# Reordering the steps of a fused attention and expert kernel before its expert work begins

## The chip, the cores and the metric

The kernel runs on one core of a Trainium2 chip. TensorE multiplies matrices into PSUM, VectorE and ScalarE work elementwise and reduce, GpSimd (POOL) does small vector work and issues some DMAs, SyncE (SP) issues the others. Each engine works through its own instructions in the order in which the program gives them, and engines wait for each other by semaphores. The metric is device time in microseconds; lower is better.

## The reference

```python
scores = scale * np.matmul(q, k.transpose(0, 1, 3, 2))
thresh = np.max(scores, axis=-1, keepdims=True) - tau
scores = np.where(scores >= thresh, scores, -1000000000.0)
scores = scores - np.max(scores, axis=-1, keepdims=True)
attn = np.exp(scores)
attn = attn / (np.sum(attn, axis=-1, keepdims=True) + 1e-09)
attn_out = np.matmul(attn, v)
x = attn_out.transpose(0, 2, 1, 3).reshape(B * S, H * D)
h = x @ w_in
out = np.maximum(0.01 * h, h) @ w_out
```

q, k and v have 8 batches, 8 heads, 576 rows and 64 columns; tau is 0.02. An attention in which only scores within tau of their row's maximum count is followed by two products (512 by 2048, 2048 by 512) with a leaky ReLU between them, the "expert" part.

## The kernel before, in words

Two heads make a pair, and two pairs a couple; there are 16 couples (c0 to c15), two to a batch. A couple is worked in 9 steps (t0 to t8) of 128 query rows for two heads. I write c1 t3 for step 3 of couple 1. One more round of 9 steps, with no attention of its own, ends the program.

What a step issues, by function:

- `s_mm(c, t)` (L158): TensorE's scores for both heads, each as three float16 products (high by high, low by high, high by low), into two tiles of two PSUM banks. There are only two such tiles, so the scores of the next step wait until this step's have been read.
- `s_max(c, t, h, direct)`: VectorE copies the negated scores of head h to SBUF and takes the row maximum (L181); POOL adds tau (L186). Then either ScalarE takes the exponential `e` (L191), and the threshold is applied later by VectorE, or, where `direct` is set, ScalarE makes the masked weights itself, in two instructions: `far` (L197), which drives values beyond the threshold far down, and an exponential into `W` with the row sum (L201).
- `s_mask(c, t)`: VectorE multiplies `e` by the threshold test (L214) for each head that was not direct, with the row sum; SP then issues the DMA that transposes `W` into `wT` (L220). It is called one step after its `s_max`. There are six `W` buffers.
- `prep(p, i)`: TensorE transposes q or k of a coming pair (L129) into the pair of banks with the tag "A", of which there is one; ScalarE makes the high half (`hi`, L138), VectorE the rest (`lo`, L139). The latter is put in a list, `soon`, and issued at the end of the step.
- `sums_0` to `sums_4`: the inverse row sums of a finished couple. POOL adds 1e-9 (L228), VectorE takes the reciprocal (L234), POOL and VectorE split it into two float16 parts (L235, L240), TensorE turns it (`sums_3`, L246) and spreads it over rows (`sums_4`, L263), each into the banks "A"; ScalarE copies the results to SBUF (`row`, L249; `rc`, L268).
- `values(c, e)`: 20 products of the transposed weights and v into the banks "A" (L279); at the end of the step VectorE multiplies by the inverse sums (L289) and POOL copies a strip (L293).

Expert work comes in units: `h_unit` (four 512-column products, L301, and the leaky ReLU on ScalarE, L305) and `out_mm` (four products with `w_out`, L316; every fourth ends a sum that ScalarE copies out). `push_main(b)` puts the 32 units of a batch in a list, 16 of the first kind and then 16 of the second. That happens at t6 of every even couple from c2 on, when the batch's second couple has been multiplied with v. `work(n)` issues the next n units. How many a step gets is computed from a table of shares and from the units and steps that remain, with a carried credit. Steps before c2 t6 have none.

POOL also issues the DMAs that load v (`load_v`) and, one per step from step 1 to 32, the slices of `w_in` and then `w_out` (`load_w`, L105 and L109); a step's number is 9c + t. SP issues the loads of q and k (L81, L86).

The order of the calls in a step, before: `s_mm`; `values` of the previous couple in t3 and t5; `s_max` of head 0, never direct; half the units; `prep`; `sums_4` in t2 and t4; `s_max` of head 1, which in couples 0 to 2 is direct except in t3 and t7; the other half of the units (in t1 `sums_1` to `sums_3` lie among these); `s_mask` of the previous step; `soon`; `sums_0` in t0; the DMAs.

Of the kernel before, what the change touches and what calls it, by code (L numbers as in the profile page):

```python
# [16 lines left out]
def kernel(  # L17
# [10 lines left out]
    nc = tc.nc  # L28
    B, H, S, D = q.shape
    tau_f = float(tau)  # L30
# [4 lines left out]
    NT = 9  # L35
# [10 lines left out]
    I16 = sb.tile([128, 128], FP16, name="I16")  # L46
# [3 lines left out]
    sel = sb.tile([128, 18, 64], FP16, name="sel")  # L50
# [19 lines left out]
    def bank():  # L70
        return ps.tile([128, 512], FP32, tag="u", bufs=2, name="u")
# [39 lines left out]
    soon = []  # L111

    def take(fs):
        r = list(fs)
        fs.clear()
        return r

    def run(fs):
        for f in fs:
            f()  # L120

    def prep(p, i, tag="A", bufs=1):
# [12 lines left out]
        N = 512 + 128 * i  # L135
        hi = sb.tile([128, N], FP16, tag=f"hi{i}", bufs=3, name=f"hi{i}")
        lo = sb.tile([128, N], FP16, tag=f"lo{i}", bufs=3, name=f"lo{i}")
        nc.scalar.activation(out=hi[:, :], in_=pt[:, 0:N], func=AF.Copy, bias=0.0, scale=QS)  # L138
        soon.append(lambda: nc.vector.scalar_tensor_tensor(  # L139
            out=lo[:, :], in0=pt[:, 0:N], scalar=QS, in1=hi[:, :],  # L140
            op0=OP.mult, op1=OP.subtract,
        ))
        qk.setdefault(p, {})[i] = (hi, lo)
# [88 lines left out]
    def sums_1(c):  # L232
        d1, rr = inv[c]
        nc.vector.reciprocal(out=rr[:, :], in_=d1[:, :])  # L234
        nc.gpsimd.tensor_scalar(out=r2[:, 0, 0:18], in0=rr[:, :], scalar1=1.0 / RS, scalar2=0.0,  # L235
                                op0=OP.mult, op1=OP.add)

    def sums_2(c):
        d1, rr = inv[c]
        nc.vector.scalar_tensor_tensor(out=r2[:, 1, 0:18], in0=rr[:, :], scalar=1.0 / RS, in1=r2[:, 0, 0:18],  # L240
                                       op0=OP.mult, op1=OP.subtract)
# [29 lines left out]
    def values(c, e):  # L271

        b, g = divmod(2 * c + e, NG)
        wT, vb = wTs[c], Vs[b % 2]
        t = pair_of_banks()
        for half in range(2):
            for kb in range(5):
                for h in range(2):
                    nc.tensor.matmul(  # L279
                        out=t[ds(h * 64, 64), half, 0:288], lhsT=vb[:, g, h, kb, :],  # L280
                        rhs=wT[:, 4 * h + kb, ds(e * 576 + half * 288, 288)],
                        start=(kb == 0), stop=(kb == 4), skip_group_check=True,
                    )
        rc = rcs.pop(e)
        x = sb.tile([128, 576], FP16, tag=f"xT{g}", bufs=2, name=f"xT{g}")
        xTs[(b, g)] = x

        def mul():
            nc.vector.tensor_tensor(  # L289
                out=x.rearrange("p (a b) -> p a b", a=2), in0=t[:, :, 0:288],  # L290
                in1=rc.rearrange("p (a b) -> p a b", a=2), op=OP.mult,
            )
            nc.gpsimd.tensor_copy(out=xE[g][:, b, :], in_=x[:, 0:64] if e else x[:, 512:576])  # L293
        soon.append(mul)
# [15 lines left out]
    def out_mm(key, g_in, part, osb, half, store):  # L310
# [9 lines left out]
        if part == 3:  # L320
# [6 lines left out]
                nc.scalar.activation(out=o[:, half, :], in_=t[:, :], func=AF.Copy, bias=0.0, scale=1.0)  # L327
            store(o)

    units = []  # L330

    def new_osb():
# [42 lines left out]
    def work(n):  # L375
        for _ in range(min(n, len(units))):
            units.pop(0)[1]()

    with tc.manual_schedule():
        nc.scalar.preload_act_table_set("natural_log_exp_and_others")  # L380
        for i, tail in ((0, 0), (1, 0), (0, 1), (1, 1)):
            load_qk(0, i, tail)
        make_identity(nc, I32)
        nc.vector.tensor_copy(out=I16[:, :], in_=I32[:, :])
        nc.vector.memset(ntau[:, :], -tau_f)
        nc.vector.memset(r2[:, :, :], 0.0)
        nc.vector.tensor_tensor(
            out=sel[:, :, :], in0=I32[:, 0:18].unsqueeze(2).to_broadcast([128, 18, 64]),
            in1=I32[:, 64:82].unsqueeze(2).to_broadcast([128, 18, 64]), op=OP.add,
        )  # L390
        nc.vector.tensor_scalar(out=sel[:, :, :], in0=sel[:, :, :], scalar1=RS, scalar2=None, op0=OP.mult)
        for t in Vs:
            nc.vector.memset(t[64:128, :, 0, 4, :], 0.0)
            nc.vector.memset(t[0:64, :, 1, 0, :], 0.0)
        for p in range(1, 3):
            for i in range(2):
                for tail in range(2):
                    load_qk(p, i, tail)
        prep(0, 0)
        prep(0, 1, "s", 2)  # L400
        run(take(soon))
        share = (23, 27, 23, 13, 23, 13, 23, 23, 23)
        credit = 0.0
        w_at = [1 + i for i in range(32)]
        prev = None
        for c in range(NC + 1):
            last = c == NC
            for t in range(NT):
                step = c * NT + t
                if c > 1 and c % 2 == 0 and t == 6:  # L410

                    if c % 4 == 2 and c > 2:
                        push_tail(c // 2 - 3, 1)
                    push_main(c // 2 - 1)
                    if c % 4 == 0:
                        push_tail(c // 2 - 2, 0)
                    if last:
                        push_tail(c // 2 - 2, 1)
                if not last:
                    s_mm(c, t)  # L420


                nxt = {6: (2 * c + 2, 0), 7: (2 * c + 2, 1), 8: (2 * c + 3, 0), 0: (2 * c + 1, 1)}
                if c == 0:
                    nxt[0], nxt[1] = (1, 0), (1, 1)
                pi = nxt.get(t)
                if pi is not None and pi[0] >= NP:
                    pi = None
                if c == 0 and t < 2:
                    prep(*pi)  # L430
                    pi = None

                if c > 0 and t in (3, 5):
                    values(c - 1, t // 2 - 1)

                ahead = [share[i % NT] for i in range(step, (c // 2 * 2 + (0 if c % 2 == 0 and t < 6 else 2)) * NT + 6)]
                credit = min(credit, 1.0) + (len(units) - credit) * share[t] / sum(ahead)
                n = min(int(credit + 0.01), len(units))
                credit -= n
                if not last:  # L440


                    direct = tau_f <= 16.0 and (
                        t not in (3, 7) if c < 3 else t in (3, 5) or not any(u[0] for u in units[:n]))
                    s_max(c, t, 0, False)
                if c > 0 and t == 1:
                    sums_1(c - 1)
                work(n - n // 2)
                if pi is not None:
                    prep(*pi)  # L450
                if c > 0 and t in (2, 4):
                    sums_4(c - 1, t // 2 - 1)
                if not last:
                    s_max(c, t, 1, direct)
                if c > 0 and t == 1:
                    sums_2(c - 1)
                    work(n // 2 - 1)
                    sums_3(c - 1)
                    work(1 if n > 1 else 0)
                else:  # L460
                    work(n // 2)
                if prev is not None:
                    s_mask(*prev)
                    prev = None
                if not last:
                    prev = (c, t)
                run(take(soon))
                if c > 0 and t == 0:
                    sums_0(c - 1)
                if c == 0 and 0 < t < 6:  # L470
                    load_v(0, t - 1)
                if c % 2 == 0 and c > 0 and t >= 4 and c // 2 < B:
                    load_v(c // 2, t - 4)
                for i in range(32):
                    if w_at[i] == step:
                        load_w(i)
                if t < 4 and 2 * c + 3 < NP:
                    load_qk(2 * c + 3, t // 2, t % 2)
                elif 4 <= t < 8 and 2 * c + 4 < NP:
                    load_qk(2 * c + 4, t // 2 - 2, t % 2)  # L480
        work(len(units))
# [35 lines left out]
```

## Time and profile before

| what | value |
|---|---|
| median of 3 runs | 539.75 us (538.6 to 540.45) |
| the profiled execution | 540.02 us, span 538.3 us |
| mean granted TensorE clock | 0.967 |
| busy: PE, DVE, ACT, POOL | 497.8, 421.7, 433.8, 188.1 us |
| start of the first maximum: c0 t0, c1 t0, c2 t0, c2 t6 | 10.13, 36.49, 64.60, 82.99 us |

The profile lists one execution. PE is TensorE's matmuls, PEld its weight loads, DVE VectorE, ACT ScalarE, SPq and POOLq the queues of SyncE and GpSimd; L181 is line 181 of the kernel, and `sn<-s` means that tile `sn` is written from tile `s`. A mark like `[0.74 <-PE s L158]` behind an instruction says that its engine sat idle for 0.74 us before it, and what ended that. A couple takes 26.36 and 28.11 us (c0, c1), then 28.68 (c2), and from c3 on 29.7 to 30.8 us.

Starts of the steps before the first expert unit, as lengths from one first maximum to the next:

| | t0 | t1 | t2 | t3 | t4 | t5 | t6 | t7 | t8 |
|---|---|---|---|---|---|---|---|---|---|
| c0 | 2.92 | 2.94 | 2.35 | 2.92 | 2.92 | 2.91 | 2.92 | 3.05 | 3.43 |
| c1 | 2.93 | 3.58 | 2.98 | 3.64 | 2.84 | 2.77 | 2.94 | 3.00 | 3.43 |
| c2 | 2.93 | 3.58 | 2.99 | 3.28 | 2.84 | 2.77 | | | |

### The profile page before, as it was taken

To read this page: it belongs to the slowest core of one execution; us is meant where nothing else is said; L and a number is where in the kernel's file an instruction comes from. 1 tells how busy PE (TensorE), PEld (TensorE's weight loads), DVE (VectorE), ACT (ScalarE), POOL (GpSimd) and SP (SyncE) were. 2 spreads that over 40 slices of the span, in tenths; PEclk is the share of its full clock that TensorE was granted. 3 is DMA by queue.
4 is the path that set the end of the run, shared out by engine and by line. 5 is a ranking of instruction groups with operands and counts; after the bars stand their busy time and mean duration, and the time that the engine had idled before them with its cause. 6 is when DMAs were issued, how large, how long until landed. Compare 5 with 4: busy or idle time off the path is not lost.

```text
span 538.3 us, 12333 instructions
## 1 busy us (share of the span) xinstructions
PE 497.8 (92%) x4384; PEld 272.8 (51%) x4384; DVE 421.7 (78%) x1106; ACT 433.8 (81%) x765; POOL 188.1 (35%) x430
## 2 busy tenths in 40 slices
PE   5678679899999999999999999999999999999996
PEld 3345454454545565454545566455545566445444
DVE  4897989988899878987899878987899878982000
ACT  3887879899878989889888989889888989884622
POOL 0754556443433334222432234323432234331000
PEclk9676969999999999999999999999999999999999
DMA  6999999998998699778999799777998699654001
GB/s 151 150 202 161 175 182 214 200 180 173 172 165 136 139 169 196 140 137 153 183 155 143 132 182 185 142 135 159 183 155 136 132 187 135 111 89 106 39 40 58
DMA packets 266814, 80.50 MB, mean 150 GB/s; under 512 B 251905, under 2 KB 264193, under 8 KB 266753
## 3 DMA queue, kind: packets, MB, share of 16 engines
q1 hardware_dynamic: 249136, 70.68, 72.3%
q0 software_dynamic: 17536, 8.92, 14.2%
q8 instruction: 34, 0.56, 0.4%
q14 instruction: 28, 0.22, 0.1%
q10 hardware_dynamic: 80, 0.13, 0.1%
HBM read 36.70 MB, written 9.44 MB: 86 GB/s over the span
## 4 chain that ended last, share of the span: by engine, by line
PE 43%; ACT 25%; DVE 16%; issue 8%; DMA 4%; POOL 3%; SPq 0%; DVEq 0%; ACTq 0%; POOLq 0%
PE u L316 13%; DVE sn L181 11%; PE u L301 10%; PE s L158 10%; PE A L279 8%; ACT e L191 7%; ACT far L197 5%; ACT W L201 5%; DVE W L214 3%; ACT gM L305 3%; ACT hi L138 3%; POOL nth L186 3%; DMA nat<-in_q_dram 2%; DVE lo L139 1%; ACT rc L268 1%
## 5 line engine op out<-in xcount | busy, mean ns | idle before, releaser
L181 DVE TENSOR_SCALAR_CACHE_REDUCE sn<-s 128x576 f32<-128x576 f32 x288 | 206.5, 750 | 49.3 <-PE s L158 49.1
L186 POOL TENSOR_SCALAR nth<-nmx 128x1 f32<-128x1 f32 x288 | 127.4, 442 | 251.7 <-DVE sn L181 229.5
L191 ACT ACTIVATE e<-sn,nmx 128x576 f16<-128x576 f32 x196 | 150.5, 769 | 32.4 <-DVE sn L181 32.2
L214 DVE SCALAR_TENSOR_TENSOR W<-sn,nth,e 128x576 f16<-128x576 f32 x196 | 155.6, 814 | 0.0
L301 PE MATMUL u<-xT,win 128*128 128x512 f16 x512 | 128.9, 380 | 2.5 <-ACT gM L305 2.5
L316 PE MATMUL u<-wout,gM 128*128 128x512 f16 x512 | 126.2, 380 | 0.0
L158 PEld LDWEIGHTS <-hi 64*128 64x128 f16 (+1 forms) x1280 | 65.1, 99 | 70.2 <-issue 54.9
L158 PE MATMUL s<-hi,hi 64*128 64x288 f16 x512 | 86.2, 300 | 10.3 <-DVE sn L181 8.8
L158 PE MATMUL s<-lo,hi 64*128 64x288 f16 (+1 forms) x640 | 92.2, 294 | 0.0
L158 PE MATMUL s<-hi,lo 64*128 64x288 f16 (+1 forms) x640 | 92.1, 294 | 0.0
L301 PEld LDWEIGHTS <-win 128*128 128x128 f16 x768 | 58.7, 98 | 56.5 <-issue 20.1
L305 ACT ACTIVATE gM<-u 128x512 f16<-128x512 f32 x128 | 74.6, 588 | 11.7 <-PE u L301 11.7
L197 ACT ACTIVATE far<-sn,nth 128x576 f32<-128x576 f32 x92 | 71.0, 771 | 13.8 <-POOL nth L186 11.6
L201 ACT ACTIVATE W<-far,ntau 128x576 f16<-128x576 f32 x92 | 71.3, 775 | 3.0
L316 PEld LDWEIGHTS <-gM 128*128 128x128 f16 x512 | 44.7, 98 | 51.3 <-issue 12.3
L139 DVE SCALAR_TENSOR_TENSOR lo<-A,hi 128x512 f16<-128x512 f32 (+1 forms) x63 | 47.6, 756 | 14.2 <-ACT hi L138 13.7
L129 PE MATMUL A<-I,nat 128*128 128x128 f32 x283 | 44.6, 288 | 9.9 <-DVE lo L139 4.7
L279 PE MATMUL A<-wT,V 128*64 128x288 f16 x640 | 47.5, 297 | 1.5 <-ACT rc L268 1.1
L129 PEld LDWEIGHTS A<-I,nat 128*128 128x128 f32 x283 | 35.2, 147 | 25.2 <-DVE lo L139 10.0
L138 ACT ACTIVATE hi<-A 128x512 f16<-128x512 f32 (+1 forms) x63 | 40.0, 636 | 7.6 <-PE A L129 7.6
L279 PEld LDWEIGHTS <-V 128*64 128x64 f16 x640 | 36.6, 113 | 11.9 <-issue 8.4
L158 PEld LDWEIGHTS <-lo 64*128 64x128 f16 (+1 forms) x640 | 32.1, 99 | 12.6 <-issue 8.9
(44 smaller groups left out, 292.1 us busy)
## 6 DMA issues: line engine op xcount, KB each, us to landing
nat<-in_q_dram SPq DMA_DIRECT2D x32, 256.0 KB, 3.8
nat<-in_k_dram SPq DMA_DIRECT2D x32, 256.0 KB, 3.9
out_dram<-osb SPq DMA_DIRECT2D x16, 512.0 KB, 3.0
wT<-W SPq DMA_TRANSPOSE x144, 3.9
V<-in_v_dram POOLq DMA_DIRECT2D x8, 256.0 KB, 6.1
win<-in_moe_w_in_dram POOLq DMA_DIRECT2D x16, 128.0 KB, 5.2
V<-in_v_dram POOLq DMA_DIRECT2D x16, 128.0 KB, 4.7
wout<-in_moe_w_out_dram POOLq DMA_DIRECT2D x16, 128.0 KB, 4.3
```

What stands on the lines that cost most here:

```text
L129: nc.tensor.matmul(out=pt[0:128, ds(c * 128, 128)], lhsT=t[0:128, 4 * i + c, :, :].rearrange("p h d -> p (h d)"), rhs=I32[:, :], is_transp ...
L158: nc.tensor.matmul(out=out[h][po, half, 0:288], lhsT=qk[p][i][a][r, cols], rhs=qk[p][1][b][r, ds(half * 288, 288)], start=(ti == 0), stop= ...
L181: nc.vector.tensor_scalar(out=sn[:, h, :].rearrange("p (a b) -> p a b", a=2), in0=s_[:, :, 0:288], scalar1=-BS, scalar2=None, op0=OP.mult, ...
L186: nc.gpsimd.tensor_scalar(out=nth[:, h:h + 1], in0=nmx[:, h:h + 1], scalar1=1.0, scalar2=tau_f, op0=OP.mult, op1=OP.add,)
L191: nc.scalar.activation(out=e[:, h, :], in_=sn[:, h, :], func=AF.Exp, bias=nmx[:, h:h + 1], scale=-1.0,)
L197: nc.scalar.activation(out=far[:, :], in_=sn[:, h, :], func=AF.Prelu, bias=nth[:, h:h + 1], scale=-1.0, alpha=BIG,)
L201: nc.scalar.activation(out=w[:, ds(h * 576, 576)], in_=far[:, :], func=AF.Exp, bias=ntau[:, 0:1], scale=1.0, accum_out=dens[c][:, 2 * t + ...
L214: nc.vector.scalar_tensor_tensor(out=w[:, ds(h * 576, 576)], in0=sn[:, h, :], scalar=nth[:, h:h + 1], in1=e[:, h, :], op0=OP.is_le, op1=OP ...
L279: nc.tensor.matmul(out=t[ds(h * 64, 64), half, 0:288], lhsT=vb[:, g, h, kb, :], rhs=wT[:, 4 * h + kb, ds(e * 576 + half * 288, 288)], star ...
L301: nc.tensor.matmul(out=t[:, ts(j, N)], lhsT=w_in16[:, gi, ts(j0 + j, 128)], rhs=xs[gi], start=(gi == 0), stop=(gi == NG - 1), skip_group_c ...
L305: nc.scalar.activation(out=g_out, in_=t[:, 0:nj * N].rearrange("p (j n) -> p j n", j=nj), func=AF.Prelu, bias=0.0, scale=1.0, alpha=0.01)
L316: nc.tensor.matmul(out=t[:, :], lhsT=g_in(j), rhs=w_out16[:, j, :], start=(j == 0), stop=(j == NJ - 1), skip_group_check=True,)
```

## The change

Steps up to c2 t3 get an order of their own ("early"); all later steps keep the old one, without the parts that belonged to the earlier couples.

- `prep` is issued right behind `s_mm`, ahead of both maxima, so that ScalarE's `hi` stands ahead of the step's exponentials.
- Head 0 is direct in every early step, head 1 never. VectorE masks one head per step.
- The chain of sums and values of couple 0 takes t0 to t4 of couple 1, that of couple 1 takes t0 to t3 of couple 2: `sums_0`; then `sums_1` and `sums_2` one behind the other; a step later `sums_3` and `sums_4` of the first pair; then `values` of the first pair; then `sums_4` and `values` of the second. `sums_3` and the second `sums_4` stand ahead of the step's maxima, the first `sums_4` and both `values` behind the mask.
- In c1 t8 the mask of that step is issued in the step itself, behind that of the step before.
- A new function, `keep_busy`, issues 5 products of 512 columns (3 in steps with a `prep`) into a bank that nobody reads, at the end of each early step but the three that hold sums and values.
- The units of batch 0 are pushed at c2 t4 instead of t6, and the shares are spread over 20 steps instead of 18. In c2 t4 to t8 head 1 is direct in t5, and elsewhere only where the step has no `h_unit`.
- The weight slices are loaded in steps 4 to 33 (two of them in steps 4 and 19) instead of 1 to 32.

```diff
+    def keep_busy(n):
+        t = bank()
+        for _ in range(n):
+            nc.tensor.matmul(
+                out=t[:, :], lhsT=I16[:, :], rhs=sel[:, 0:8, :].rearrange("p a b -> p (a b)"),
+                start=True, stop=True, skip_group_check=True,
+            )
...
-        w_at = [1 + i for i in range(32)]
+        w_at = [4 + 94 * i // 100 for i in range(32)]
...
-                if c > 1 and c % 2 == 0 and t == 6:
+                if c > 1 and c % 2 == 0 and t == (4 if c == 2 else 6):
...
+                early = c < 2 or c == 2 and t < 4
+                if early:
+                    u = t - (0 if c == 2 else 1) if c > 0 else None
+                    if pi is not None:
+                        prep(*pi)
+                    if u == 1:
+                        sums_3(c - 1)
+                    if u == 3:
+                        sums_4(c - 1, 1)
+                    s_max(c, t, 0, tau_f <= 16.0)
+                    s_max(c, t, 1, False)
+                    if prev is not None:
+                        s_mask(*prev)
+                    prev = (c, t)
+                    if c == 1 and t == 8:
+                        s_mask(*prev)
+                        prev = None
+                    if c == 1 and t == 0 or c == 2 and t == 0:
+                        sums_0(c - 1)
+                    if u == 0:
+                        sums_1(c - 1)
+                        sums_2(c - 1)
+                    if u == 1:
+                        sums_4(c - 1, 0)
+                    if u in (2, 3):
+                        values(c - 1, u - 2)
+                    run(take(soon))
+                    if u not in (1, 2, 3):
+                        keep_busy(5 if pi is None else 3)
...
-                ahead = [share[i % NT] for i in range(step, (c // 2 * 2 + (0 if c % 2 == 0 and t < 6 else 2)) * NT + 6)]
+                    ahead = [share[i % NT] for i in range(
+                        step, (c // 2 * 2 + (0 if c % 2 == 0 and c > 2 and t < 6 else 2)) * NT + 6)]
...
-                    direct = tau_f <= 16.0 and (
-                        t not in (3, 7) if c < 3 else t in (3, 5) or not any(u[0] for u in units[:n]))
+                        direct = tau_f <= 16.0 and (t in (3, 5) or not any(u[0] for u in units[:n]))
```

More of the change, by code (lines that the diff above doesn't have):

```diff
@@ L428 @@
                     pi = None
[L429 to L434, printed above, removed]
-                ahead = [share[i % NT] for i in range(step, (c // 2 * 2 + (0 if c % 2 == 0 and t < 6 else 2)) * NT + 6)]
-                credit = min(credit, 1.0) + (len(units) - credit) * share[t] / sum(ahead)
-                n = min(int(credit + 0.01), len(units))
-                credit -= n
@@ L440 @@
-                if not last:
-                    direct = tau_f <= 16.0 and (
-                        t not in (3, 7) if c < 3 else t in (3, 5) or not any(u[0] for u in units[:n]))
[L445 to L459, printed above, removed]
-                else:
[L461 to L469, printed above, removed]
+                early = c < 2 or c == 2 and t < 4
@@ new lines @@
+                if early:
[26 more added lines that the diff above has]
+                        keep_busy(5 if pi is None else 3)
+                else:
+                    if c > 2 and t in (3, 5):
+                        values(c - 1, t // 2 - 1)
+                    ahead = [share[i % NT] for i in range(
+                        step, (c // 2 * 2 + (0 if c % 2 == 0 and c > 2 and t < 6 else 2)) * NT + 6)]
+                    credit = min(credit, 1.0) + (len(units) - credit) * share[t] / sum(ahead)
+                    n = min(int(credit + 0.01), len(units))
+                    credit -= n
+                    if not last:
+                        direct = tau_f <= 16.0 and (t in (3, 5) or not any(u[0] for u in units[:n]))
+                        s_max(c, t, 0, False)
+                    if c > 2 and t == 1:
+                        sums_1(c - 1)
+                    work(n - n // 2)
+                    if pi is not None:
+                        prep(*pi)
+                    if c > 2 and t in (2, 4):
+                        sums_4(c - 1, t // 2 - 1)
+                    if not last:
+                        s_max(c, t, 1, direct)
+                    if c > 2 and t == 1:
+                        sums_2(c - 1)
+                        work(n // 2 - 1)
+                        sums_3(c - 1)
+                        work(1 if n > 1 else 0)
+                    else:
+                        work(n // 2)
+                    if prev is not None:
+                        s_mask(*prev)
+                        prev = None
+                    if not last:
+                        prev = (c, t)
+                    run(take(soon))
+                    if c > 2 and t == 0:
+                        sums_0(c - 1)
```

## The prediction

> **What bounds the kernel now.** I read the slices first, then busy time by stage, then the engines' instructions in order of time inside the first stage. The page's slices, 13.5 us each, come first.
>
> ```profile
> PE   5678679899999999999999999999999999999996
> ...
> PEclk9676969999999999999999999999999999999999
> ```
>
> Nearly all of TensorE's idle time, and all of its reduced clock, lies in the first nine slices. The stretches are cut at the start of steps c0 t0, c1 t0, c2 t0 and c2 t6 (the first step with an expert unit); columns: length, then PE, PEld, DVE, ACT, POOL busy, clock, DMA share, GB/s.
>
> ```profile
> 10.13:36.49 26.36, 19.74 (x143) 11.29 (x142) 23.75 (x62) 21.16 (x36) 15.48 (x31) 0.74 1.13 166
> 36.49:64.60 28.11, 19.29 (x190) 12.10 (x190) 25.14 (x67) 22.56 (x40) 14.10 (x31) 0.82 1.18 177
> 64.60:82.99 18.39, 14.33 (x132) 9.10 (x133) 16.03 (x45) 14.40 (x26) 9.67 (x21) 0.72 1.07 187
> 82.99:142.67 59.68, 56.47 (x508) 29.78 (x507) 51.14 (x135) 53.99 (x99) 27.71 (x61) 1.00 1.11 183
> 142.67:484.00 341.33, 334.13 (x3083) 182.85 (x3083) 296.87 (x781) 297.98 (x528) 118.67 (x274) 1.00 0.88 152
> ```
>
> From 83 us TensorE is busy 95 to 98%: there the time is its work. Before that no engine is full; the limit is a loop, seen in two neighbouring steps of VectorE:
>
> ```profile
> 15.99 0.75 DVE L181 TENSOR_SCALAR_CACHE_REDUCE sn<-s 128x576 f32<-128x576 f32 x1
> ...
> 18.34 0.76 DVE L181 TENSOR_SCALAR_CACHE_REDUCE sn<-s 128x576 f32<-128x576 f32 x1 [0.17 <-PE s L158]
> 19.02 0.08 DVE L181 DVE_READ_ACCUMULATOR sn<-s 128x1 f32 x1
> 19.02 0.76 DVE L181 TENSOR_SCALAR_CACHE_REDUCE sn<-s 128x576 f32<-128x576 f32 x1
> ...
> 21.26 0.76 DVE L181 TENSOR_SCALAR_CACHE_REDUCE sn<-s 128x576 f32<-128x576 f32 x1 [0.74 <-PE s L158]
> ```
>
> Two maxima (0.68 us apart) free the score banks, then TensorE computes the next scores. With the clock up a step takes 2.35 us (15.99 to 18.34), with it halved 2.92 (18.34 to 21.26). ScalarE's row for the direct mask follows.
>
> ```profile
> 18.24 0.78 ACT L197 ACTIVATE far<-sn,nth 128x576 f32<-128x576 f32 x1
> 19.05 0.77 ACT L201 ACTIVATE W<-far,ntau 128x576 f16<-128x576 f32 x1
> 19.73 0.18 ACT L201 ACTIVATION_READ_ACCUMULATOR W<-far,ntau 128x1 f32 x1
> 19.82 1.42 ACT L191 ACTIVATE e<-sn,nmx 128x576 f16<-128x576 f32 x2
> ```
>
> Spacings: far 0.80, W 0.87 with its accumulator read, e 0.67: one direct and one indirect head cost 2.34 us of ScalarE per step, as much as the 2.35 us loop.
>
> **The change, part by part.** I write S for the start of a step's first maximum. Up to c2 t3 every step now has head 0 direct, head 1 by e and a mask. Head 0's maximum ends at S+0.76, the threshold takes 0.19 (POOL's row beside a maximum; 0.70 beside a mask), so far starts at S+1.1, W at 1.9, e at 2.77, ending at S+3.44. That is 1.1 us into the next step. ScalarE is thus always half a step behind VectorE, and it matters in three places below.
>
> *c0 t0 and t1.* Three fillers come after each prep. A 512-column product costs 0.215 us (four in 0.86). With the clock low I take 0.43, because the 288-column pairs go from 0.12 apart to 0.24. At t0 the clock is low until about 14.4: 3 x 0.43 = 1.3 us in front of the next scores, of which VectorE's own order hides 0.3. **+1.0.**
> *c0 t2 to t5.* Before 2.35 + 3 x 2.92 = 11.1. Five fillers (1.08) fit in the 1.42 us that TensorE waits for the two maxima and keep it 85% busy, so the clock stays. ScalarE and the loop both give 2.36; I take 2.38, 9.5 in all. **-1.6.** If the fillers failed to hold the clock, it would be 0.
> *c0 t6 to c1 t0, four preps.* Before 12.33. VectorE: 1.36 maxima + 0.74 mask + 0.61 or 0.74 lo; ScalarE: 2.34 + 0.5 to 0.6 hi: 2.75, 2.88, 2.75, 2.95 = 11.33 (t7's second mask is gone). **-1.0.**
> *c1 t1, t2.* Before 3.58 + 2.98. The reciprocal and its rounding are now back to back: VectorE waits for one POOL result (0.3) but TensorE's turn, a step later, no longer waits ahead of the scores. 2.97 + 2.40. **-1.2.**
> *c1 t3 to t5.* The row sums' copy to SBUF (rc, 0.63) is issued after e in t2, so on ScalarE it ends 1.7 us into t3. Values need the same pair of banks, so they start at S+1.76; behind them, in TensorE's order, wait the next scores and all of VectorE's next step. Clock up: 1.76 + 1.35 (20 products) + 0.9 scores = 4.0; t4 (sums 0.42, rc 0.63, values 1.35, scores 0.9) 3.4; t5 2.4. Sum 9.8. Clock halved: values 2.4, scores 1.5, five fillers 2.1: 12.9 if it lasts. Before: 9.25. There are no fillers here, and between the scores of t2 and the values TensorE has 1.6 us of work (0.27 + 0.42 + 0.9) in 4.8. The nearest row is c1 t1 of before, TensorE in order of time and then the stretches around it:
>
> ```profile
> 38.48 0.53 PE L158 MATMUL s<-lo,hi 64*128 64x288 f16 x2
> 41.12 0.29 PE L246 MATMUL A<-I,r 128*128 128x128 f16 x1 [2.11 <-DVE r L240]
> ```
>
> ```profile
> 31.30:41.10 9.80, 5.10 (x58) 3.11 (x57) 9.67 (x28) 8.22 (x14) 4.86 (x12) 0.85 1.25 240
> 41.10:48.50 7.40, 6.58 (x50) 4.17 (x50) 5.06 (x14) 6.09 (x11) 3.65 (x7) 0.50 1.16 171
> ```
>
> After an idle stretch of 2.11 us the clock was 0.50 for 7.4 us. So I take 11.9, nearer to the low clock. **+2.6** (0.5 to 3.7).
> *c1 t6, t7.* 5.94 to 5.63. **-0.3.**
> *c1 t8: couple 1's own last mask at once.* It waits for e of its own step: ScalarE hi, far, W, e end at S+4.2. The mask ends at 5.0, lo of the next prep behind it at 5.62, and only then the next maximum. Before 3.43. **+2.2.** TensorE meanwhile waits 3.2 us for lo to free the transposes' banks.
> *c2 t0.* No mask is left (-0.74), but the chain POOL, reciprocal, POOL, rounding stands on VectorE ahead of lo (3.5 in all), and with the clock low transposes 1.26 + fillers 1.29 + scores 1.5 give 4.05. Before 2.93. **+1.1** (0.6 to 1.1).
> *c2 t1 to t3.* As in couple 1: 2.4 + 4.0 + 3.4 = 9.8 at full clock, 12.3 at half; 11.0 taken, as TensorE comes in busy from t0. Before 9.85. **+1.1** (0 to 2.5).
> *c2 t4, t5, now with a unit each.* Masks on VectorE bind; 5.4 for 5.61. **-0.2.**
> Start of c2 t6: 1.0 - 1.6 - 1.0 - 1.2 + 2.6 - 0.3 + 2.2 + 1.1 + 1.1 - 0.2 = **+2.7**, between +0.5 and +5.
>
> *Two units done early.* The shares give one unit in t4, one in t5, and 30 instead of 32 up to c4 t5. 2 x 0.86 us of TensorE, of which the share that it is busy there (56.47 of 59.68) counts: **-1.6** (-1.0 to -1.7).
> *The weight loads.* SP's order keeps its DMAs; POOL's loads of weights now end in step 33 instead of 32, while the output unit that reads the last slices moves from step 35 to 34. Before, issue at 113.53 and use at 119.44 were 5.9 us apart; the time to landing of these loads (L109):
>
> ```profile
> DMA to landing us min/median/max: 3.2/4.3/6.8
> ```
>
> Now the issue is at S+2.2 of c3 t6, the use at S+4.1 (a step of 3.3, then three products). TensorE waits 1.3 to 4.9, by the median 2.4, in a stretch where it is the bound: **+2.4** (0 if landing is quicker than any row).
>
> Sum: 2.7 - 1.6 + 2.4 = +3.5. The profiled execution took 540.02 (span 538.3 and 1.7 around it), 0.27 above the median 539.75; 543.5 there is **543.2** as a median.
>
> **The rivals.**
> *The clock stays up in the chains* (fillers just before them, none within). c1 t3 to t5 then cost +0.5 and c2 t1 to t3 nothing: +0.5 - 1.6 + 2.4 = +1.3, **541.0**, no change. For it: 48.5 to 66 us had the clock at 0.99 with TensorE busy 67%. Against: the 2.11 us row. The Trainium skill, page TensorE: Matmul & The Clock Gate, section "Why this matters for your kernels", asks for no idle gap over about 3 us; by that rule the gaps of 1.8 us here would keep the clock, and this rival would hold. The trace disagrees: 2.11 us preceded 0.50.
> *Faster: ScalarE is not behind.* If e of head 1 ends by the second maximum (S+1.4), t8's mask waits for nothing (-2.9), values start 1.4 sooner twice, and c2 t0 loses its low clock (-0.55): 0.5 - 2.9 - 2.8 - 0.55 = -5.8, and -5.0 in all, **534.7**. It decides where ScalarE's step is under about 2.0 us. For it: ScalarE was busy only 80% in couple 0. Against: 0.80 + 0.87 + 0.67 leaves it no slack to catch up with.
> *Slower still: the turning DMAs of W are late.* SP issued almost without a pause from 19.6 to 77 us; couple 0's last transfer was issued at 39.91 and by the median of 5.0 landed at 44.9, where values could now start at 45.0. At the longest landing, 9.0, values wait 3.9 us; once such a wait gives **547.1**. Against: three fewer weight loads share the engines in couple 0.
>
> **How the numbers follow.** Forecast (543.2, its own range 541.5 to 546.5) 0.45; clock stays up 0.20; faster 0.20; late DMAs 0.15. A measurement of this kernel can tell about 0.3%, 1.6 us. Faster: 0.20 and a tenth of the clock's case, if the last weights also land in time (538.6 or less): 0.22. Within: 0.18. Slower: 0.60. The range 536 to 548 leaves out most of the faster rival (about 0.13) and the far end of the late DMAs (0.05).
>
> **What would show it.** Right: c0 t2 to t5 at 2.4 us a step with the clock at 1.00; values in c1 t3 idle until ScalarE's rc; a mask in c1 t8 that starts 4 us after the step, with a TensorE gap near 3 us; a wait of an output unit for a weight DMA in c3 t7; c2 t6 starting at 83.5 to 88 us. Wrong: rc ending near the start of the values' step, full clock throughout, or c2 t6 before 82 us.

## The result

The changed kernel takes 547.1 us (median of 4 runs, 544.39 to 548.07) against 540.1 before: a ratio of 1.0125 with a 95% interval of 1.0082 to 1.0169. It is slower by 1.25%, some 7 us. The forecast was 543.2; its own range was 541.5 to 546.5, and the whole range, with rivals in it, 536 to 548. An interval in this document is worked out from the executions within 1.5% of their kernel's quickest, which leaves out four of six in run 8 and one each in runs 9, 10 and 11. The profiled execution took 547.64 us with a span of 545.9. First the page's slices after the change, 13.6 us each:

```profile
PE   5987769898999999999999999999999999999996
...
PEclk9986989998999999999999999999999999999999
```

The clock is indeed up in the second, third and sixth slice, where it was at 0.6 to 0.7. But the fourth is still at 0.6, TensorE is busy only 0.6 to 0.7 in the fourth to sixth, and the tenth (123 to 136 us) has dropped to 0.8 in both rows. The stretches by stage, cut at the same steps as before (c0 t0, c1 t0, c2 t0, c2 t6, c4 t6; columns as before: length, PE, PEld, DVE, ACT, POOL busy, clock, DMA share, GB/s):

```profile
10.19:36.62 26.43, 24.00 (x178) 12.39 (x177) 22.15 (x57) 22.17 (x39) 13.50 (x29) 0.94 1.06 148
36.62:69.14 32.52, 24.35 (x212) 14.93 (x212) 24.58 (x65) 24.74 (x46) 14.15 (x32) 0.84 1.14 189
69.14:88.22 19.08, 15.12 (x143) 9.07 (x144) 15.71 (x43) 14.82 (x26) 10.33 (x24) 0.91 0.96 150
88.22:149.86 61.64, 55.88 (x500) 29.55 (x499) 52.53 (x140) 51.25 (x91) 27.02 (x60) 0.97 1.04 172
```

In the first microseconds the clock column is too high: it reads 1.00 up to about 15 us, though the three fillers of c0 t0 take 1.49 us there and those of c0 t1 0.81. So couple 0's clock in this row is somewhat too high.

Couple 0 takes 26.43 us instead of 26.36 although its clock rose from 0.74 to 0.94. Couple 1 takes 32.52 instead of 28.11. c2 t6 starts at 88.22, which is 5.23 later than before, and the next 18 steps lose another 1.96 (61.64 against 59.68) although they hold two units less. From c4 t6 to the end another 0.4 is added. Lengths of the steps that tell it, in us:

| | before | after |
|---|---|---|
| c0 t0 | 2.92 | 4.09 |
| c0 t2 to t5 | 2.35, 2.92, 2.92, 2.91 | 2.32, 2.32, 2.32, 2.33 |
| c0 t6, t7 | 2.92, 3.05 | 4.13, 3.33 |
| c1 t3, t4, t5 | 3.64, 2.84, 2.77 | 5.96, 5.42, 2.32 |
| c1 t8, c2 t0 | 3.43, 2.93 | 5.35, 4.05 |
| c2 t1, t2, t3 | 3.58, 2.99, 3.28 | 2.33, 4.05, 3.48 |
| c3 t5, t7 | 4.25, 3.23 | 3.51, 6.39 |

Besides c0 t0, where the fillers stand ahead of the scores, four places lose. **The values** of couple 1 and couple 2, TensorE in order of time:

```profile
46.32 2.61 PE L279 MATMUL A<-wT,V 128*64 128x288 f16 x20 [1.69 <-ACT rc L268]
...
77.28 1.42 PE L279 MATMUL A<-wT,V 128*64 128x288 f16 x20 [1.69 <-ACT rc L268]
```

Both wait 1.69 us for ScalarE's copy `rc`; c1 t3 starts at 44.56, so the first begins at S+1.76. The same products then take 2.61 us in couple 1 and 1.42 in couple 2. The clock is the reason, as the stretches around the first show:

```profile
39.00:46.30 7.30, 4.07 (x36) 2.20 (x36) 6.82 (x20) 6.88 (x14) 4.26 (x11) 0.94 1.30 185
46.30:55.40 9.10, 8.35 (x68) 6.09 (x69) 4.14 (x10) 5.05 (x9) 2.23 (x6) 0.50 1.14 208
```

TensorE is busy for 8.35 of 9.10 us there at half clock, and VectorE for less than half of it. **The mask at once** in c1 t8, first VectorE, then ScalarE and TensorE:

```profile
67.80 0.82 DVE L214 SCALAR_TENSOR_TENSOR W<-sn,nth,e 128x576 f16<-128x576 f32 x1 [1.83 <-issue]
...
66.95 0.76 ACT L191 ACTIVATE e<-sn,nmx 128x576 f16<-128x576 f32 x1
...
69.28 1.30 PE L129 MATMUL A<-I,nat 128*128 128x128 f32 x5 [3.11 <-DVE lo L139]
```

The step started at 63.79; its mask waits until 67.80, just behind ScalarE's `e` of the same step, which ended at 67.71 (the profile itself names no releaser here). The transposes of c2 t0, which need `lo` behind it, start after 3.11 idle us of TensorE and then run at half clock (1.30 us for five). **POOL's loads in c0 t4**, POOL's own rows and then ScalarE's:

```profile
24.03 0.64 POOL L96 DMA_DIRECT2D V<-in_v_dram  x1
24.67 1.12 POOL L105 DMA_DIRECT2D win<-in_moe_w_in_dram  x2
25.87 0.70 POOL L186 TENSOR_SCALAR nth<-nmx 128x1 f32<-128x1 f32 x2
...
26.33 0.78 ACT L197 ACTIVATE far<-sn,nth 128x576 f32<-128x576 f32 x1 [1.06 <-POOL nth L186]
```

The load of v and two weight slices hold POOL for 1.76 us, the threshold of c0 t5 (its maximum ended at 24.83) comes out of it at about 26.2, and the direct mask, which now stands first in the step on ScalarE, waits for it. In c0 t6 VectorE's mask then waits 1.34 us for the delayed ScalarE. **The last weight slices** in c3 t7:

```profile
122.67 0.38 PE L316 MATMUL u<-wout,gM 128*128 128x512 f16 x1 [0.84 <-DMA wout<-in_moe_w_out_dram]
124.55 0.59 PE L316 MATMUL u<-wout,gM 128*128 128x512 f16 x1 [1.50 <-DMA wout<-in_moe_w_out_dram]
```

2.34 us of waiting, and the products behind it run at half clock until about 127.3 (0.59 for one that took 0.38).

### The profile page after: what moved, and what is told of

Read it like the earlier page. It is cut to its first block, busy times and chain, and to the rows that moved or that the text cites. A ratio compares the mean times of both kernels' runs of the same rounds, so it can differ in the third digit from the quotient of the medians.

```text
span 545.9 us, 12450 instructions
## 1 busy us (share of the span) xinstructions
PE 507.5 (93%) x4444; PEld 276.1 (51%) x4444; DVE 420.5 (77%) x1102; ACT 435.7 (80%) x769; POOL 187.8 (34%) x430
## 4 chain that ended last, share of the span: by engine, by line
PE 45%; ACT 25%; DVE 15%; issue 9%; POOL 3%; DMA 2%; SPq 0%; DVEq 0%; POOLq 0%; ACTq 0%
PE u L316 13%; PE u L301 10%; PE s L158 10%; DVE sn L181 9%; PE A L279 8%; ACT e L191 6%; ACT far L197 5%; ACT W L201 5%; DVE W L214 3%; ACT gM L305 3%; ACT hi L138 3%; POOL nth L186 3%; DVE lo L139 2%; PE A L129 1%; ACT rc L268 1%
## 5 line engine op out<-in xcount | busy, mean ns | idle before, releaser
L158 PEld LDWEIGHTS <-hi 64*128 64x128 f16 (+1 forms) x1280 | 61.8, 99 | 69.8 <-issue 54.8
L158 PE MATMUL s<-hi,lo 64*128 64x288 f16 (+1 forms) x640 | 87.8, 291 | 0.0
L158 PE MATMUL s<-lo,hi 64*128 64x288 f16 (+1 forms) x640 | 87.5, 290 | 0.0
L158 PE MATMUL s<-hi,hi 64*128 64x288 f16 x512 | 81.3, 293 | 3.6 <-DVE sn L181 2.0
L197 ACT ACTIVATE far<-sn,nth 128x576 f32<-128x576 f32 x94 | 72.5, 771 | 15.2 <-POOL nth L186 13.5
L201 ACT ACTIVATE W<-far,ntau 128x576 f16<-128x576 f32 x94 | 72.9, 775 | 3.1
L279 PEld LDWEIGHTS <-V 128*64 128x64 f16 x640 | 37.8, 113 | 15.0 <-issue 12.0
L327 ACT ACTIVATE osb<-u 128x512 f32<-128x512 f32 x35 | 20.5, 586 | 24.4 <-PE u L316 24.2
```

The source lines that it names most:

```text
L158: nc.tensor.matmul(out=out[h][po, half, 0:288], lhsT=qk[p][i][a][r, cols], rhs=qk[p][1][b][r, ds(half * 288, 288)], start=(ti == 0), stop= ...
L197: nc.scalar.activation(out=far[:, :], in_=sn[:, h, :], func=AF.Prelu, bias=nth[:, h:h + 1], scale=-1.0, alpha=BIG,)
L201: nc.scalar.activation(out=w[:, ds(h * 576, 576)], in_=far[:, :], func=AF.Exp, bias=ntau[:, 0:1], scale=1.0, accum_out=dens[c][:, 2 * t + ...
L279: nc.tensor.matmul(out=t[ds(h * 64, 64), half, 0:288], lhsT=vb[:, g, h, kb, :], rhs=wT[:, 4 * h + kb, ds(e * 576 + half * 288, 288)], star ...
```

## The experiments

My theory, called the order theory in the expectations: the fillers do what they should, and the loss sits in single waits that the new order makes. Its rivals differ by run. All runs were compared with the kernel before, on the same chip; "after" is the changed kernel. Where a run's own executions lie far apart, I give their spread. A turning DMA is the DMA that transposes `W` into `wT` (L220). Each run was profiled in one execution only.

**1. The last mask a step later.**

```diff
-                if c > 1 and c % 2 == 0 and t == (4 if c == 2 else 6):
+                if c > 1 and c % 2 == 0 and t == (5 if c == 2 else 6):
-                early = c < 2 or c == 2 and t < 4
+                early = c < 2 or c == 2 and t < 5
-                    u = t - (0 if c == 2 else 1) if c > 0 else None
+                    u = t - 1 if c > 0 else None
-                    if c == 1 and t == 8:
-                        s_mask(*prev)
-                        prev = None
```

> Couple 1's last mask goes back to the step after it, its chain starts one step later (t1 to t4 of couple 2, as couple 0's does in couple 1) and the units of batch 0 begin at c2 t5. Order theory (the loss sits in single waits that the new order makes): c1 t8 falls from 5.35 to about 2.75 us and c2 t0 from 4.05 to about 2.85; the gain of 3.8 is given back in part by the chain's extra step and one unit less ahead (0.9), and by whatever clock the chain in couple 2 then has: 543.5 with the clock up, 547 if it falls to half there as in couple 1. Rival (the early steps are bound by ScalarE's sum of work, so that a wait removed shows up elsewhere): c1 t8 gets shorter, c2 t0 and t1 longer by as much, 546.5 to 548.

541.61 us (539.15 to 543.67), ratio to before 1.0022 [1.0005, 1.0040]. c1 t8 took 2.69 and c2 t0 2.82, so the rival falls: the wait did not come back elsewhere. But the chains changed their clocks. Values of couple 1 and of couple 2 in this run:

```profile
44.82 1.42 PE L279 MATMUL A<-wT,V 128*64 128x288 f16 x20 [1.69 <-ACT rc L268]
...
71.23 2.61 PE L279 MATMUL A<-wT,V 128*64 128x288 f16 x20 [2.03 <-ACT rc L268]
```

Now it is couple 1 that keeps the clock after an idle gap of 1.69 us, the very gap after which the changed kernel lost it, and couple 2 that loses it (c2 t3 and t4 took 6.30 and 5.44). Some 1.3 us of this run's gain lies ahead of the edit: couple 0 took 25.14 us instead of 26.43, by c0 t0 (3.37) and c0 t7 (2.83).

**2. rc ahead of the maxima.**

```diff
                     if u == 1:
                         sums_3(c - 1)
+                        sums_4(c - 1, 0)
...
-                    if u == 1:
-                        sums_4(c - 1, 0)
```

> The first copy of the row sums (rc) is issued ahead of the step's maxima, so on ScalarE ahead of far, W and e; TensorE's order is untouched. Order theory: values of c1 t3 start within 0.3 us of the step's first maximum instead of 1.76, the clock stays up, c1 t3 and t4 fall from 5.96 and 5.42 to about 3 and 3.4, c2 t2 from 4.05 to about 3: 541 to 543. Rival (ScalarE's sum of work binds): exponentials come 0.6 us later, the next mask waits for them, and less than 1.5 us is gained: 545.5 to 547.

542.66 us (540.74 to 543.87), 1.0052 [1.0035, 1.0068]. c1 t3 and t4 fell from 5.96 and 5.42 to 3.77 and 3.42, and c2 t2 from 4.05 to 2.96 (c2 t1 grew from 2.33 to 3.00). The first values start at once, but the second half of them now waits for something else:

```profile
44.25 0.80 PE L279 MATMUL A<-wT,V 128*64 128x288 f16 x10
...
46.35 0.80 PE L279 MATMUL A<-wT,V 128*64 128x288 f16 x10 [1.29 <-DMA wT<-W]
```

A turning DMA has not landed. That is the rival I had called "slower still", behind the wait that I took away.

**3. Fillers in the chain.**

```diff
                     if u == 1:
+                        keep_busy(2)
                         sums_3(c - 1)
+                        keep_busy(2)
...
                     if u in (2, 3):
+                        keep_busy(6 if u == 2 else 3)
                         values(c - 1, u - 2)
```

> Fillers also in the chain's steps: two before and two behind the turned sums, six and three ahead of the two values. They fill TensorE's waits (0.54, 0.54, 1.7, 0.7 us) and change no other engine's order. If the low clock there is what makes c1 t3 and t4 long (5.96 and 5.42), they fall to about 4.0 and 3.4 with the clock at 1.00, couple 2 stays as it is: about 543. If it is the waits and not the clock, both steps stay over 5 us or grow by the fillers' 1.3 us: 547 to 549.

543.27 us (541.33 to 547.19), 1.0069 [1.0031, 1.0107]. Six fillers and then the values, and the stretch that was at half clock in the changed kernel:

```profile
44.65 1.47 PE L334 MATMUL u<-sel,I 128*128 128x512 f16 x6
...
46.40 1.42 PE L279 MATMUL A<-wT,V 128*64 128x288 f16 x20 [0.28 <-ACT rc L268]
```

```profile
46.30:55.40 9.10, 8.71 (x96) 5.61 (x96) 7.30 (x19) 7.22 (x14) 4.53 (x10) 1.00 1.25 191
```

The values still wait for `rc`, only with products in the gap. c1 t3 and t4 took 4.04 and 3.49 instead of 5.96 and 5.42. So 3.85 us of what the changed kernel loses in couple 1 is the clock alone; the wait itself, now filled, is still 1.7 us of c1 t3.

**4. The weight loads of before.**

```diff
-        w_at = [4 + 94 * i // 100 for i in range(32)]
+        w_at = [1 + i for i in range(32)]
```

> The weight slices are loaded in steps 1 to 32 as before, nothing else is undone. Order theory: the wait for the last slice in c3 t7 goes (6.39 to about 3.2 us), and c0 t6 falls from 4.13 to about 3.0, since POOL no longer issues three loads between two thresholds in c0 t4; 542.5 to 543.5. Rival (POOL's load of v alone makes the threshold late, and the slices' wait hides another that is as long): c0 t6 stays over 4, c3 t7 falls by less than 1.5: 545.5 to 547.

546.76 us (545.41 to 548.57), 1.0126 [1.0102, 1.0150]: no gain, where I expected 4 us. Both places behaved nearly as the order theory says (c0 t6 3.25 us, c3 t7 4.20 with 1.1 us of waiting left). Couple 0 took 23.91 us, but 1.07 of that gain is c0 t0, which took 3.02 because the clock came up within its fillers (1.14 us for three, 1.49 in the changed kernel), and not because of the loads. Then c1 t2 took 5.05 and c1 t3 6.35. ScalarE in c1 t1, and SP in couple 0:

```profile
40.89 0.77 ACT L201 ACTIVATE W<-far,ntau 128x576 f16<-128x576 f32 x1 [1.93 <-DMA wT<-W]
```

```profile
29.22 7.34 SPq L220 DMA_TRANSPOSE wT<-W  x1
```

One turning DMA occupied SP for 7.34 us, the six buffers of `W` ran out, and the direct mask had to wait for one. In this run the loads of v and of the weights go out side by side in a couple 0 of 2.3 us a step; that this is what made the DMA slow is a guess that no run shows (the fifth one took 4.80 us in the kernel before, with the same loads, and 5.78 in the changed kernel). The Trainium skill says, in Trainium Kernel Development and Optimization, section "Key Constraints", that DMAs from SP, ScalarE and POOL run on the same 16 engines and interleave. The trace is in keeping with that, but it does not show what the 7.34 us were spent on. By the totals (546.76 against 547.1) the later loads of the changed kernel cost at the end about what they save here.

**5. No fillers.**

```diff
-                        keep_busy(5 if pi is None else 3)
+                        pass
```

> All fillers are left out, nothing else. Clock theory (they keep the clock up where the step is a loop of scores and maxima): c0 t0 falls from 4.09 to about 3.0, c0 t2 to t5 rise from 2.32 to about 2.9 each, couple 2's chain is also at half clock (c2 t2 about 6): 548 to 551. Rival (fillers only stand in front of scores, the steps being bound by ScalarE's 2.34 us): c0 t2 to t5 stay near 2.4: 545 to 546.

548.63 us (545.23 to 550.28), 1.0146 [1.0113, 1.0179]. c0 t0 fell to 2.92, c0 t2 to t5 rose to 2.75, 2.92, 2.92, 2.92, and couple 2's chain went to half clock (0.50 from 69 to 84 us; c2 t2 and t3 4.94 and 5.28). The clock theory holds. But couple 0 as a whole took 25.87 us, less than the 26.43 with fillers: at 2.92 us a step POOL is in time, and c0 t6 takes 2.92 instead of 4.13.

**6. The kernel before with fillers alone.**

```diff
                 run(take(soon))
+                if step < 24 and not (c > 0 and 0 < t < 6):
+                    keep_busy(5 if t in (2, 3, 4, 5) else 3)
```

> The kernel before with the fillers alone (five in t2 to t5 and three in t0, t1 and t6 to t8 of couple 0; three in t0 and t6 to t8 of couple 1, none in t1 to t5 of couples 1 and 2). Clock theory: c0 t2, t4 and t5 near 2.4 instead of 2.35, 2.92, 2.91, c0 t0 about 4.0 instead of 2.92 if its fillers run at half clock; the chain of couple 1 as before or better. Start of c2 t6 about 81 to 83 (82.99 before): 537.5 to 540. If the order and not the clock sets the steps before: 540 to 541, steps unchanged.

543.04 us (540.22 to 545.14), 1.0047 [1.0019, 1.0076]: slower than without, which neither reading expected. The stretch of couple 0 and the second half of the values of c1 t3:

```profile
10.04:36.25 26.21, 22.35 (x178) 11.68 (x177) 23.47 (x61) 21.17 (x36) 15.49 (x31) 1.00 1.13 132
```

```profile
49.81 0.80 PE L279 MATMUL A<-wT,V 128*64 128x288 f16 x10 [2.62 <-DMA wT<-W]
```

From c0 t1 on couple 0 runs at full clock (0.74 without fillers), and it takes 26.21 us instead of 26.36: c0 t3 and t5 fall to 2.3 us, but c0 t0 takes 3.80, since its fillers run at half clock ahead of the scores (1.49 us for three), and c0 t6 3.40. In c1 t3 the values wait 2.62 us for a turning DMA (6.13 us instead of 3.64). The turning DMAs came later than in the kernel before, though the couple was hardly quicker: the third and the fifth occupied SP for 5.70 and 6.72 us, where they had taken 3.56 and 4.80. Why they took longer is open. A quicker loop in couple 0 alone thus brought nothing.

**7. Weight loads from 6 to 31.**

```diff
-        w_at = [4 + 94 * i // 100 for i in range(32)]
+        w_at = [6 + i if i < 16 else 22 + (i - 16) * 9 // 15 for i in range(32)]
```

> Of the changed kernel only the weight loads are moved: one per step from step 6 (behind the last load of v), the second half in steps 22 to 31. Order theory, with what the run that loaded them from step 1 added (there W waited for late turning DMAs): c0 t6 from 4.13 to about 2.8, since no two loads stand between thresholds in c0 t4; no wait for turning DMAs in couple 1; c3 t7 from 6.39 to about 3.2. Couple 1's chain still at S+1.76 and at half clock or full: 542.5 at half, 539 at full. Rival (the turning DMAs are late whenever couple 0 is quick): c1 t2 or t3 grows by 1 to 3 us, 544 to 546.

550.58 us (547.32 to 554.29), 1.0192 [1.0149, 1.0235]. c0 t6 fell to 3.08 and c3 t7 to 3.67, as the order theory says, and couple 0 took 24.80. The chains of couples 1 and 2 both fell to half clock (c1 t3 5.32, c2 t2 and t3 5.96 and 5.35). But c3 t3 took 11.30 us; from the list of TensorE's waits:

```profile
PE A L279 <- DMA wT<-W: 6.1, 1, 6.1
```

**8. Four parts together:** those loads, the mask of run 1, the `rc` of run 2, and no fillers in c0 t0 and t1.

```diff
-                    if u not in (1, 2, 3):
+                    if u not in (1, 2, 3) and step > 1:
                         keep_busy(5 if pi is None else 3)
```

> Those loads; couple 1's last mask a step later and its chain from t1 on; rc ahead of the maxima; no fillers in c0 t0 and t1. Order theory: c0 in 23.3 to 24, couple 1 in 25.7 to 27 (values of t3 may wait 1.3 us for a turning DMA, as in the run with rc early), c2 t0 to t4 in 14.5, so c2 t6 starts at 76 to 78 instead of 82.99 and one unit is done by then: 533 to 535. Rival (ScalarE's sum of work binds the early steps): c2 t6 not before 81: 538 or more.

The executions lie between 534.64 and 551.12 us, median 543.97; the two quickest alone would give 0.9926. In the profiled one (544.8), couple 0 took 23.63, couple 1 25.50, and c2 t6 started at 78.24 instead of 82.99: the early steps do what the order theory says. Then c3 t3 took 13.37 us. SP and TensorE:

```profile
86.96 9.23 SPq L220 DMA_TRANSPOSE wT<-W  x1
```

```profile
108.11 1.41 PE L279 MATMUL A<-wT,V 128*64 128x288 f16 x10 [7.86 <-DMA wT<-W]
```

**9 and 10. The mended orders with other loads.** Run 9 is run 8 with the changed kernel's loads and with fillers in the chain (two before and two behind `sums_3`, three ahead of the second values); run 10 differs from it by this line.

```diff
-        w_at = [4 + 94 * i // 100 for i in range(32)]
+        w_at = sorted(list(range(5, 32)) + [9, 11, 13, 15, 17])
```

> The changed kernel's own weight loads (steps 4 to 33), with the orders mended as in the run with four parts undone, and fillers in the chain's steps (two before and two behind the turned sums, three ahead of the second values). Theory (turning DMAs were late in c3 t3 because two weight slices a step went out beside the loads of v; one a step is borne): no wait over 2 us for a turning DMA, c2 t6 starts at 76.5 to 79, c3 t7 still waits some 3 us for the last slice: 535 to 537. Rival (a quick start alone makes the turning DMAs late): c3 t3 again over 8 us, 541 or more.

> The same, with the weight loads in steps 5 to 31 and the five that are left over in c1 t0, t2, t4, t6 and t8, where no v is loaded. Theory: as the run beside it, but without the wait in c3 t7 (6.3 to about 3.2 us) and with c0 t6 near 2.9: 532 to 534. Rival (any step with two slices makes turning DMAs late): a wait of 2 us or more for them in couple 1's or couple 2's chain, 536 to 541.

Run 9: 537.08 us (five executions at 536.01 to 538.57, one at 547.53), 0.9940 [0.9924, 0.9957] without that one. Run 10: 539.61 (534.53 to 542.96), 0.9976 [0.9953, 0.9999] without its longest. The ones left out waited for turning DMAs, as the rows below show, so they belong to these kernels: with them the means are 538.8 and 539.1 us against 540.1 before, and no gain is sure. The profiles caught the longest execution of each, and in both it is c3 t3 again (11.34 and 10.05 us). From TensorE's waits, run 9 and then run 10:

```profile
PE A L279 <- DMA wT<-W: 6.7, 2, 5.8
```

```profile
PE A L279 <- DMA wT<-W: 7.1, 2, 5.3
```

In run 9 the weights go out one slice a step at that place, so "two slices a step" cannot be what makes the turning DMAs late there; my theory of these two runs falls. In run 10 c0 t6 fell to 3.07 and c3 t7 to 3.24, as it said, and a turning DMA was also late in c1 t3 (5.00).

**11 and 12. Batch 1's v in couple 1.** Run 11 is run 9 with this; run 12 has the loads of run 7 besides.

```diff
-                if c % 2 == 0 and c > 0 and t >= 4 and c // 2 < B:
+                if c == 1 and t < 5:
+                    load_v(1, t)
+                if c % 2 == 0 and c > 2 and t >= 4 and c // 2 < B:
                     load_v(c // 2, t - 4)
```

> The mended orders with the changed kernel's weight loads (4 to 33), and batch 1's v loaded in c1 t0 to t4 (steps 9 to 13) instead of c2 t4 to t8: the same bytes, earlier. If the turning DMAs of couple 2 are late in c3 t3 because v, weights and turning DMAs share the engines in c2 t4 to t8, that wait goes (11.3 to about 3.5 us) and the runs lie close together, 534.5 to 537, with the last slice's wait of some 3 us in c3 t7 still there; the price may be a wait of 1 to 3 us in couple 1's chain. If the early stage as a whole has too little DMA time, the wait only moves: c1 t3 or c2 t3 over 6 us and a median over 537.

> The same, with the weight loads of the run that had two slices a step in steps 22 to 31. If v beside them was what made c3 t3 long, it is near 3.5 us now, c3 t7 is near 3.2 (no wait for a slice) and the time is 532 to 534.5. If two slices a step are enough to make turning DMAs late, c3 t3 stays over 8 us and the time over 538.

Run 11: 542.25 us (537.03 to 545.97), 1.0018 [0.9989, 1.0047]. c3 t3 is short (3.51), but c2 t3 takes 10.37 and c1 t3 4.84: the wait has moved to the chain before. Run 12: 538.37 us (535.06 to 540.93), 0.9953 [0.9931, 0.9975]. Its profile is of its quickest execution; TensorE's waits for `wT`, and then the early stages:

```profile
PE A L279 <- DMA wT<-W: 3.4, 2, 1.8
```

```profile
9.88:33.42 23.54, 20.75 (x172) 11.15 (x171) 22.09 (x57) 21.82 (x39) 11.56 (x26) 1.00 1.05 153
33.42:60.70 27.28, 21.90 (x219) 12.39 (x219) 23.94 (x64) 23.53 (x44) 16.32 (x37) 1.00 1.31 209
60.70:78.49 17.79, 15.05 (x148) 8.38 (x149) 15.62 (x42) 15.68 (x29) 9.18 (x23) 1.00 1.17 179
```

All three stages are at full clock, c2 t6 starts at 78.49, 4.5 us earlier than before, c3 t3 takes 3.51 and c3 t7 3.25. Moving v thus takes the wait out of c3 t3 in both profiled executions, even with two slices a step. In run 11 turning DMAs were late in c1 t3 and c2 t3 instead; in run 12 the waits there were 1.84 and 1.56 us. As run 12's profile is of its quickest execution, it does not show where the slower ones (up to 540.93) lost time. Why run 12 was spared in c2 t3 where run 11 was not is open: their loads are the same through most of couple 1.

Run 12 beats the kernel before by about 0.5% with an interval clear of 1, and the changed kernel by 1.6% (538.37 against 547.1, not timed side by side). It is the only one of the twelve whose gain over the kernel before is clear with every execution counted; five of run 9's six are quicker than any of the kernel before on the same chip.

## Why the prediction was right, and where it was not

The sign was right, and so were the waits that the prediction named: `rc` behind `e`, couple 1's last mask, the last weight slices. The total (543.2 against 547.1) was too low. It lies beyond the forecast's own range and within 548 only because the stated range made room for late turning DMAs, which did not come; that this rival's figure was 547.1 is chance. Three terms were too small by 4.3 us together (c0 t6 to c1 t0, c1 t3 to t5, c3 t7), and one too large by 1.1 (c2 t1 to t3). By its own steps, predicted and measured in us:

| step | predicted | measured |
|---|---|---|
| c0 t0, t1 | +1.0 | +1.1 |
| c0 t2 to t5 | -1.6 | -1.8 |
| c0 t6 to c1 t0 | -1.0 | +0.7 |
| c1 t1, t2 | -1.2 | -1.5 |
| c1 t3 to t5 | +2.6 | +4.5 |
| c1 t6, t7 | -0.3 | -0.4 |
| c1 t8 | +2.2 | +1.9 |
| c2 t0 | +1.1 | +1.1 |
| c2 t1 to t3 | +1.1 | 0.0 |
| c2 t4, t5 | -0.2 | -0.4 |
| two units early | -1.6 | -1.6 |
| last weight slices, c3 t7 | +2.4 | +3.2 |

The measured column adds up to 6.8 us; the profiled span grew by 7.6, and the other 0.8 is spread over later steps and not explained.

- *c0 t0, t1*: the size is partly luck. With the same order c0 t0 took 4.09 us here and 3.02 in run 4, by when the clock rose.
- *c0 t6 to c1 t0* is the step that failed in kind. I followed ScalarE and VectorE there and set POOL's part of the start (far at S+1.1) without POOL's loads in front of the next threshold, though I had named the loads for the end of the weights. The rows show 1.76 us of loads, and ScalarE idle for 1.06 us ahead of far. Run 7, which spares c0 t4 the weight slices, gets c0 t6 to 3.08 and the four steps to 11.42, close to the 11.33 forecast.
- *c1 t3 to t5*: the wait was right to the hundredth (S+1.76), the clock was mis-sized. I took a value near the half clock; it was at half for two whole steps, and +4.5 is beyond the upper end that I gave. That end was itself too low, by 0.8: at half clock values and scores took 2.54 and 1.66 us in t3 where I had 2.4 and 1.5, and in t4 the values began at S+1.29 where my terms give 1.05. In couple 2 the clock held and the term was 0 instead of +1.1. Run 3 separates the two: with the gaps filled, c1 t3 to t5 take 9.86 (4.04 + 3.49 + 2.33), +0.6, the low end of my bounds.
- *c1 t8 and c2 t0*: right in place, mechanism and size; run 1 undoes both.
- *Two units*: c3 t5 and c4 t5, the steps with a unit less, fell by 0.74 and 0.86.
- *Last slices*: 2.34 us of idle time as forecast; the rest is the half clock after it, which I had not counted.

The rival "the clock stays up" came true in one chain of two, couple 2's. By the gap rule of the Trainium skill that I had cited (TensorE: Matmul & The Clock Gate, "Why this matters for your kernels") it should have in both: a gap of 1.69 us was followed by half clock in c1 of the changed kernel and by full clock in its c2 and in c1 of run 1. The same page, under "What's actually happening", says that the window over which activity is judged runs free; that would let equal gaps end differently, and these rows agree with it, though no run here shows the window.

The rival "faster: ScalarE is not behind" fails by run 2: with `rc` early, the values start at once, but c1 t8 still takes 5.35 us, so ScalarE's half step stays. "Late DMAs" did not decide here; the changed kernel's only wait for `wT` is one weight load's, of 0.2 us. (Its argument against them was off by one: couple 0 holds 6 weight loads instead of 8, two fewer and not three.) It is what often comes next: in the profiles of runs 2, 4 and 6 to 12 TensorE's longest wait for a turning DMA is 1.3 to 7.9 us. Not always, though: run 1, quicker in couples 0 and 1 than the kernel before, has none over 0.6 us. What makes these DMAs late stays open. Run 9 shows that it does not take two slices a step, and run 11 that loading v elsewhere can move the wait.

## What to carry to other kernels

When a step is made quicker, look for what was hidden behind the old step: here POOL's DMA issues had fitted into 2.92 us and did not fit into 2.32, and waits for the turning DMAs, of which the profile of the kernel before has none, came up in most of the quicker versions. A small copy that frees a shared buffer (rc) belongs ahead of the long work of its engine: that took c1 t3 and t4 from 11.38 to 7.19 us (run 2), where holding the clock with the wait left in place took them to 7.53 (run 3). The two gains overlap: with the early copy the clock stayed at 1.00 there too. Here fillers were worth their place only in gaps: ahead of waiting work at half clock they cost 1.17 us (c0 t0), and inside the chain's waits they gave 3.85 us.

## What the runs showed of the hardware that I had not expected

- The turning DMAs' time is far from fixed: one occupied SP for 1.24 to 9.23 us, and landing took up to 16.6 us in run 8, beside 3.2 to 9.0 in the kernel before. The executions of run 8 differed by up to 16.5 us, where those of the kernel before, on any one chip, lie within about 3; that late turning DMAs make the whole difference is not shown, as only one of the six was profiled.
- An equal idle gap of TensorE (1.69 us) was followed by full or by half clock.
- Full clock from c0 t1 on in couple 0 (run 6) shortened it by only 0.15 us net: what c0 t3 and t5 gained, the fillers of c0 t0 at half clock and c0 t6 gave back.
